# Early chunks load into their own memory, alternate their output banks, and share VectorE with weight conversion in another order

## The chip, the cores and the metric

The kernel runs on one core of one Trainium2 chip. The metric is the device time of one execution in microseconds; the time before is the median of three runs. A profile is one execution recorded by the hardware profiler.

## The reference

All arithmetic must have float32 quality; the weights and vectors of the two dense layers arrive as float64 and are taken apart on the chip.

```python
def _attn_ref(q, k, v, lam):                 # (2, 8, 768, 64), causal decay lam per head
    for b in range(nb):                      # the kernel uses blocks of 128 in place of 64
        intra = einsum('bhic,bhjc->bhij', qb, kb) * Dmask
        intra = einsum('bhij,bhjd->bhid', intra, vb)
        inter = einsum('bhid,bhde->bhie', qb * lam_pow, kv_state)
        out[:, :, sl] = intra + inter
        kv_state = lam_block * kv_state + einsum('bhsd,bhse->bhde', kb * rev_pow, vb)

x = attn_out as 1536 tokens x 512
h = x @ w_in;  x = (h * clip(h + 3, 0, 6) / 6) @ w_out          # layer 1, 512 -> 2048 -> 512
h = x @ w_in;  g = P(h) / (Q(h) + 1e-6);  out = g @ w_out        # layer 2, same shapes
```

## The kernel before, in words

The attention is cut into 12 chunks of 128 tokens (6 to each batch entry). For chunk c, `att_t` transposes q and k on TensorE into two PSUM banks and ScalarE copies them out as qT and kT; GpSimd makes qd (q times its decay) and kd (k times its decay). `att_s` multiplies k by q into two banks, and VectorE multiplies the result by the decay mask into `at`. `att_o` gathers the chunk's output in bank X from state times qd (not in the first chunk of a batch entry) and from at times v, and the new state's addition in bank Y. `att_state` adds that addition to the decayed state on VectorE, and GpSimd makes the decayed copy sd. `att_x` splits the output into a high part xh (ScalarE) and a rest xl (VectorE), both read from bank X.

A dense layer multiplies with weights that are split in the same way into a high part (wih, woh) and a rest (wil, wol). A job of weight conversion has one or two halves of 128x512: `load_job` fetches the raw float64 words; `conv_c` scales on ScalarE (L153) and clips on VectorE (L154); `conv_s` scales the low words on ScalarE (L176) and joins them on VectorE (L177); `conv_w` puts the sign in on VectorE (L194); `conv_h` makes the high part on ScalarE (L207) and the rest on GpSimd (L208). Jobs 0 and 1 have one half each (the weights of `mm1(0)` and `mm1(1)`), and every later job has two: the first half of job 2 is the weight of `mm1(2)`.

`mm1(s)` is 12 TensorE multiplications of 512 columns into hb, of xh by wih (L216), xh by wil (L218) and xl by wih (L220); `act1` (tc on ScalarE, td on VectorE) and `act_fin` (gh on ScalarE, gl on GpSimd) turn it into the input of `mm2(s)`, of four quarters with three multiplications each. The program first does chunks 0 to 3, which fill the first 512 tokens, then the scores of chunk 4 and `mm1(0)`, and then eight steps s = 0 to 7, each of which weaves chunk 4+s into the first layer; then the dense layers alone. The order of the work on each engine is written out by hand, and each engine takes its instructions strictly in that order. Loads wait in SyncE's queue, also in order, until the buffer that they fill is free: q, k and v have two buffers each, raw words two of each kind.

Of the kernel before, what the change touches and what calls it, by code (L numbers as in the profile page):

```python
# [8 lines left out]
F32 = mybir.dt.float32  # L9
# [11 lines left out]
WARM = (6, 2, 3)  # L21
# [9 lines left out]
def fused_kernel(  # L31
# [52 lines left out]
    EIN, EOUT = 11, 9  # L84
    w_tiles(wp, range(EIN), range(EOUT))
# [223 lines left out]
    with ExitStack() as actx:  # L309
        ap = actx.enter_context(tc.tile_pool(name="ap", bufs=1))  # L310
# [13 lines left out]
        def load_nat(c, which):  # L324
            b, s0 = c // CPB, (c % CPB) * CH
            for nm in which:
                x = ap.tile([128, H, D], F32, name=nm + "n", bufs=2)
                src = {"q": q, "k": k, "v": v}[nm]
                nc.sync.dma_start(x, src[b, :, s0 : s0 + CH, :].rearrange("h s d -> s h d"))
                nat.setdefault(c, {})[nm] = x  # L330

        def att_t(c, bk, between=None):
            qn, kn, vn = (nat[c][nm] for nm in "qkv")
# [11 lines left out]
            nc.scalar.copy(kT.rearrange("p a b -> p (a b)"), bk[1])  # L345
            qd = kd = None
# [24 lines left out]
        Xv = X.rearrange("p (a b) -> p a b", a=NP)  # L371
        Yd = Y[:, 0 : 64 * NP].rearrange("p (a b) -> p a b", a=NP)
        decayed = {}

        def att_o(c):
            at, qd, kd, vn = live[c]
            cs = [slice(128 * p, 128 * p + 128) for p in range(NP)]

            if qd is not None:
                for p in range(NP):  # L380
                    nc.tensor.matmul(X[:, cs[p]], lhsT=state[:, p, :], rhs=qd[:, p, :], start=p == 0, stop=False,
# [6 lines left out]
            for p, h2, r in halves:  # L388
                nc.tensor.matmul(X[r, cs[p]], lhsT=vn[:, 2 * p + h2, :], rhs=at[:, h2, p, :],
                                 start=qd is None and p == 0, stop=p == NP - 1, skip_group_check=True)  # L390

        def att_state(c):
            if c % CPB == CPB - 1:
                return
            for h2 in range(2):
# [12 lines left out]
        def att_x(c):  # L408
            del live[c]
            o = CH * (c % CPT)  # L410
# [5 lines left out]
        with tc.manual_schedule():  # L416
            load_nat(0, "qk")
            nc.scalar.dma_start(lamb, lam.unsqueeze(0).to_broadcast([128, H]))
            load_nat(1, "qk")
            load_nat(0, "v")  # L420
            nc.vector.memset(warm, 0.0)
# [11 lines left out]

            warm_up(WARM[0])
            for h2 in range(2):
                r = slice(64 * h2, 64 * h2 + 64)
                nc.vector.tensor_copy(lamq[r, :], lamb.rearrange("p (a b) -> p a b", b=2)[r, :, h2])
            for p in range(NP):
# [3 lines left out]
                for h2 in range(2):  # L442
                    hd = 2 * p + h2
                    nc.vector.tensor_tensor_scan(
                        out=dmat[:, h2, p, :], data0=lamb[:, hd : hd + 1].to_broadcast([128, CH]), data1=ident,
                        initial=0.0, op0=ALU.mult, op1=ALU.add)
            for h2 in range(2):
                nc.vector.tensor_copy(ktab[:, :, h2], dmat[:, h2, :, CH - 1])
# [4 lines left out]


            att_t(0, hb, lambda: warm_up(WARM[1]))
            warm_up(WARM[2])
            load_nat(2, "qk")
            load_nat(1, "v")
            att_s(0, acc[0:2])
            load_job(0)  # L460
            att_t(1, hb)
            att_o(0)
            att_state(0)
            att_x(0)
            load_nat(2, "v")
            load_nat(3, "qk")
            load_job(1)
            att_s(1, acc[2:4])
            att_t(2, hb)
            conv_all(conv_c, 0)  # L470
            conv_all(conv_s, 0)
            conv_all(conv_w, 0)
            att_o(1)
            att_state(1)
            att_x(1)
            conv_all(conv_h, 0)
            load_nat(3, "v")
            load_nat(4, "qk")
            load_job(2)
            att_s(2, acc[0:2])  # L480
            att_t(3, hb)
            conv_all(conv_c, 1)
            conv_all(conv_s, 1)
            conv_all(conv_w, 1)
            att_o(2)
            att_state(2)
            att_x(2)
            conv_all(conv_h, 1)
            load_nat(4, "v")
            load_job(3)  # L490
            load_nat(5, "qk")
# [153 lines left out]
```

## Time and profile before

| what | value |
|---|---|
| three runs, median (lowest to highest) | 602.6 us (602.4 to 602.93) |
| the profiled execution's own time | 602.82 us |
| its span in the profile | 600.9 us, so 1.92 us lie around it |
| TensorE's busy share | 98% |
| granted TensorE clock, mean | 1.0 of full speed |

The span runs from the first to the last record; the time of the execution lies 1.92 us above it. A busy share is an average over the whole span; the change touches the first 115 us or so.

### The profile page before, as it was taken

The page shows a single profiled execution, that of the slowest core. Times are in us where ns is not written, and L with a number is a line of the kernel's source. Part 1 is how long each engine was busy: PE and PEld are TensorE (multiplying, and loading weights), DVE is VectorE, ACT ScalarE, POOL GpSimd, SP SyncE. Part 2 cuts the span into 40 slices and gives each one's busy share as a digit, 9 for nine tenths or more (in the row PEclk, how much of TensorE's full clock was granted, in tenths as well). Part 3 has the DMA queues.
Part 4 walks back from the last instruction along what each step waited for, and adds up shares of the span by engine and source line. Part 5 has one row for each costly group of instructions (what it writes and reads, how often), then busy time and mean ns, then how long its engine had stood idle before and what let it go on. Part 6 is the DMA issues. An engine that isn't in the chain of part 4 may idle for free.

```text
span 600.9 us, 8288 instructions
## 1 busy us (share of the span) xinstructions
PE 588.1 (98%) x3035; PEld 480.6 (80%) x3035; DVE 445.2 (74%) x476; ACT 384.0 (64%) x635; POOL 366.8 (61%) x291
## 2 busy tenths in 40 slices
PE   8898999999999999999999999999999999999997
PEld 5786888888888888888888787877788888888886
DVE  5877888787411011488888899999999888999991
ACT  2566465677422222588787877787887767877771
POOL 3756677566421222266676677688776677777772
PEclk9999999999999999999999999999999999999999
DMA  8987755364000000266655000000010000100001
GB/s 169 267 214 196 173 157 160 130 211 150 1 1 0 1 0 1 88 206 197 184 171 172 1 1 35 1 0 2 28 43 0 2 0 2 69 2 0 1 1 71
DMA packets 61289, 46.68 MB, mean 78 GB/s; under 512 B 39104, under 2 KB 55744, under 8 KB 61248
## 3 DMA queue, kind: packets, MB, share of 16 engines
q1 hardware_dynamic: 60960, 46.02, 26.9%
q8 instruction: 24, 0.39, 0.3%
q10 hardware_dynamic: 288, 0.14, 0.1%
q14 instruction: 17, 0.14, 0.1%
HBM read 43.00 MB, written 3.15 MB: 77 GB/s over the span
## 4 chain that ended last, share of the span: by engine, by line
PE 52%; DVE 24%; ACT 4%; issue 3%; POOL 1%; DVEq 0%; ACTq 0%
PE acc L235 26%; DVE Y L304 8%; PE hb L216 8%; PE hb L220 8%; PE hb L218 8%; DVE ta L154 2%; DVE X L164 2%; DVE ta L194 2%; DVE Y L164 2%; DVE tb L294 2%; DVE tb L194 2%; ACT ta L153 1%; DVE td L305 1%; DVE tb L154 1%; DVE raw L184 1%
## 5 line engine op out<-in xcount | busy, mean ns | idle before, releaser
L304 DVE RECIPROCAL Y<-tb 128x512 f32<-128x512 f32 x48 | 161.3, 3360 | 1.6
L281 POOL TENSOR_TENSOR gl<-td,gh 128x512 fp32r<-128x512 f32 x84 | 111.2, 1324 | 77.1 <-ACT gh L280 76.0
L216 PE MATMUL hb<-xh,wih 128*128 128x512 f32 x384 | 104.3, 393 | 0.5 <-ACT td L293 0.4
L218 PE MATMUL hb<-xh,wil 128*128 128x512 f32 x384 | 102.7, 389 | 0.0
L220 PE MATMUL hb<-xl,wih 128*128 128x512 f32 x384 | 102.6, 389 | 0.0
L295 POOL TENSOR_TENSOR tc<-ta,tc 128x512 f32<-128x512 f32 x48 | 62.2, 1295 | 58.2 <-ACT tc L292 58.2
L271 DVE SCALAR_TENSOR_TENSOR td<-tc,hb 128x512 f32<-128x512 f32 x48 | 32.8, 683 | 84.3 <-ACT tc L268 84.3
L216 PEld LDWEIGHTS hb<-xh,wih 128*128 128x128 f32 x384 | 71.1, 188 | 17.4 <-ACT td L293 1.8
L218 PEld LDWEIGHTS hb<-xh,wil 128*128 128x128 f32 x384 | 72.1, 188 | 15.2
L220 PEld LDWEIGHTS hb<-xl,wih 128*128 128x128 f32 x384 | 72.1, 188 | 15.0
L268 ACT ACTIVATE tc<-hb,c 128x512 f32<-128x512 f32 x48 | 32.9, 686 | 71.7 <-PE hb L220 71.6
L235 PE MATMUL acc<-gh,woh 128*128 128x512 f32 x192 | 76.1, 396 | 0.0
L235 PE MATMUL acc<-gl,woh 128*128 128x512 f32 x192 | 74.8, 390 | 0.0
L235 PE MATMUL acc<-gh,wol 128*128 128x512 f32 x192 | 74.8, 389 | 0.0
L280 ACT CAST gh<-td 128x512 fp32r<-128x512 f32 x84 | 52.0, 619 | 25.9 <-DVE td L271 13.8
L296 POOL TENSOR_TENSOR td<-td,tc 128x512 f32<-128x512 f32 x48 | 63.8, 1330 | 3.8
L208 POOL TENSOR_TENSOR wil<-ta,wih 128x512 fp32r<-128x512 f32 x32 | 41.4, 1294 | 34.7 <-ACT wih L207 34.7
L289 ACT ACTIVATE X<-hb,b_sb 128x512 f32<-128x512 f32 x48 | 31.8, 662 | 42.8 <-PE hb L220 34.1
L235 PE MATMUL acc<-woh,gl 128*128 128x512 f32 x144 | 56.5, 392 | 1.1 <-POOL gl L281 1.1
L235 PE MATMUL acc<-woh,gh 128*128 128x512 f32 x144 | 56.2, 390 | 0.3 <-ACT raw L253 0.3
L235 PE MATMUL acc<-wol,gh 128*128 128x512 f32 x144 | 56.0, 389 | 0.0
L208 POOL TENSOR_TENSOR wol<-tb,woh 128x512 fp32r<-128x512 f32 x29 | 38.4, 1324 | 14.4 <-ACT woh L207 14.4
(104 smaller groups left out, 1029.1 us busy)
## 6 DMA issues: line engine op xcount, KB each, us to landing
raw<-in_moe_w_in_dram SPq DMA_DIRECT2D x32, 512.0 KB, 3.8
raw<-in_moe_w_out_dram SPq DMA_DIRECT2D x32, 512.0 KB, 4.6
qn<-in_q_dram SPq DMA_DIRECT2D x12, 256.0 KB, 5.5
kn<-in_k_dram SPq DMA_DIRECT2D x12, 256.0 KB, 5.3
vn<-in_v_dram SPq DMA_DIRECT2D x12, 256.0 KB, 4.8
out_dram<-raw SPq DMA_DIRECT2D x11, 256.0 KB, 2.2
out_dram<-raw ACTq DMA_DIRECT2D x1, 128.0 KB, 1.8
out_dram<-raw SPq DMA_DIRECT2D x1, 128.0 KB, 1.7
```

The lines of the kernel that those rows point to most:

```text
L208: nc.gpsimd.tensor_tensor(lo, x, hi.bitcast(F32), op=ALU.subtract)
L216: nc.tensor.matmul(h, lhsT=ih[:, kk, :], rhs=xh[tb][:, kk, :], start=kk == 0, stop=False)
L218: nc.tensor.matmul(h, lhsT=il[:, kk, :], rhs=xh[tb][:, kk, :], start=False, stop=False)
L220: nc.tensor.matmul(h, lhsT=ih[:, kk, :], rhs=xl[tb][:, kk, :], start=False, stop=kk == KD - 1)
L235: nc.tensor.matmul(acc[d], lhsT=l, rhs=r, start=st and i == 0, stop=sp and i == 2)
L268: nc.scalar.activation(t, h, AF.Relu, bias=c3)
L271: nc.vector.scalar_tensor_tensor(out=g, in0=t, scalar=6.0, in1=h, op0=ALU.min, op1=ALU.mult)
L280: nc.scalar.copy(gh, g)
L281: nc.gpsimd.tensor_tensor(gl, g, gh.bitcast(F32), op=ALU.subtract)
L295: nc.gpsimd.tensor_tensor(b1, h2, b1, op=ALU.mult)
L296: nc.gpsimd.tensor_tensor(a1, a1, b1, op=ALU.add)
L304: nc.vector.reciprocal(Y, q1)
```

## The change

Three things are altered. The natural q, k and v of chunks 0 to 3 get a buffer each, in a pool `pp` whose memory the weights wi5 to wi10 take over later, so that none of these loads waits for a buffer; they are issued at once, with the raw words of jobs 0 and 1 between them. `att_o` gets its banks as an argument: chunks 0 to 3 put their output alternately into X and Y and into acc[2] and acc[3], and all scores of the early chunks use acc[0] and acc[1]. The order written by hand is altered: jobs 0 to 2 are converted later, in single steps between a chunk's own steps; in the steps s the order becomes `att_x` before `att_state`, only one half of `conv_s` before them, and `conv_w` of a job in the following step, after td and ahead of at. The counts of the start's dummy multiplications (WARM) go from 6, 2, 3 to 8, 3, 2.

```diff
-WARM = (6, 2, 3)
+WARM = (8, 3, 2)
...
-    EIN, EOUT = 11, 9
-    w_tiles(wp, range(EIN), range(EOUT))
+    EARLY, EIN, EOUT = 5, 11, 9
+    w_tiles(wp, range(EARLY), range(EOUT))
+    pre = ExitStack()
+    pp = pre.enter_context(tc.tile_pool(name="pp", bufs=1))
...
-                x = ap.tile([128, H, D], F32, name=nm + "n", bufs=2)
+                if c < CPT:
+                    x = pp.tile([128, H, D], F32, name=f"{nm}n{c}")
+                else:
+                    x = ap.tile([128, H, D], F32, name=nm + "n", bufs=2)
...
-        def att_o(c):
+        def att_o(c, bk=(X, Y)):
...
             load_nat(0, "qk")
             nc.scalar.dma_start(lamb, lam.unsqueeze(0).to_broadcast([128, H]))
-            load_nat(1, "qk")
             load_nat(0, "v")
+            load_nat(1, "qkv")
+            load_nat(2, "qkv")
+            load_job(0)
+            load_nat(3, "qkv")
+            load_job(1)
+            load_nat(4, "qk")
...
+            S, O = acc[0:2], ((X, Y), acc[2:4])
+            slots = {
+                2: ((conv_c, 0), (conv_s, 0)),
+                3: ((conv_w, 0), (conv_c, 1)),
+            }
+            for c in range(CPT):
+                att_s(c, S)
+                att_t(c + 1, hb)
+                for f, j in slots.get(c, ())[0:1]:
+                    conv_all(f, j)
+                att_o(c, O[c % 2])
+                if c < CPT - 1:
+                    att_d(c + 1)
+                    att_state(c)
+                else:
+                    conv_all(conv_h, 0)
+                    att_state(c)
+                    att_d(c + 1)
+                for f, j in slots.get(c, ())[1:2]:
+                    conv_all(f, j)
+                att_x(c)
...
+            conv_all(conv_s, 1)
+            load_nat(6, "qk")
+            att_s(CPT, S)
+            conv_all(conv_w, 1)
+            conv_all(conv_h, 1)
+            load_job(3)
...
                 if s == 0:
                     mm1(0)
                     act1(0)
+                    conv_all(conv_c, 2)
+                    conv_s(2, 0)
                     att_o(c)
-                    att_state(c)
                     att_x(c)
+                    att_state(c)
+                    conv_s(2, 1)
+                    conv_all(conv_w, 2)
                     act_fin(0)
-                    conv_all(conv_c, j)
-                    conv_all(conv_s, j)
+                    conv_all(conv_h, 2)
...
+                    att_d(c)
+                    conv_all(conv_w, j - 1)
+                    conv_all(conv_h, j - 1)
...
                     conv_all(conv_c, j)
-                    conv_all(conv_s, j)
+                    conv_s(j, 0)
                     mm2(s - 1, (2, 3))
                     att_o(c)
-                    att_state(c)
                     att_x(c)
-                    conv_all(conv_w, j)
+                    att_state(c)
+                    conv_s(j, 1)
```

The part of `att_t` that made qd and kd is now the function `att_d`, and the new pool that holds wi5 to wi10 opens after `pre.close()`.

On VectorE, this is the place from the scores of chunk 4 to the sign step of job 2 (ta and tb are the two halves of a job), before the change:

```order
L366 TENSOR_TENSOR at<-acc_78,dmat 128x512
L366 TENSOR_TENSOR at<-acc_79,dmat 128x512
L398 TENSOR_TENSOR state<-sd,Y 64x4x64 x2
L414 TENSOR_TENSOR xl_87<-X,xh_84 128x4x128
L154 TENSOR_SCALAR ta<-ta 128x512
L154 TENSOR_SCALAR tb<-tb 128x512
L177 SCALAR_TENSOR_TENSOR ta<-ta,raw_340 128x512
L177 SCALAR_TENSOR_TENSOR tb<-tb,raw_342 128x512
L366 TENSOR_TENSOR at<-acc_76,dmat 128x512
L366 TENSOR_TENSOR at<-acc_77,dmat 128x512
L194 SCALAR_TENSOR_TENSOR ta<-raw_340,ta 128x512
L194 SCALAR_TENSOR_TENSOR tb<-raw_342,tb 128x512
```

It runs from chunk 3's at to job 2's sign steps. After the change, from job 1's sign step (raw_167) on, it reads:

```order
L196 SCALAR_TENSOR_TENSOR ta<-raw_167,ta 128x512
L273 SCALAR_TENSOR_TENSOR td<-tc,hb_80 128x512
L156 TENSOR_SCALAR ta<-ta 128x512
L156 TENSOR_SCALAR tb<-tb 128x512
L179 SCALAR_TENSOR_TENSOR ta<-ta,raw_327 128x512
L426 TENSOR_TENSOR xl_88<-X,xh_85 128x4x128
L409 TENSOR_TENSOR state<-sd,Y 64x4x64 x2
L179 SCALAR_TENSOR_TENSOR tb<-tb,raw_329 128x512
L196 SCALAR_TENSOR_TENSOR ta<-raw_327,ta 128x512
L196 SCALAR_TENSOR_TENSOR tb<-raw_329,tb 128x512
```

Job 2 (raw_327, raw_329) now stands behind td of `mm1(0)`, and chunk 4's xl and state (xl_88) stand inside it.

On ScalarE at the same place, after the change; wih_92 is job 1's high part, wih_94 that of job 2, hb_80 the result of `mm1(0)` and hb_81 that of `mm1(1)`:

```order
L209 CAST wih_92<-ta 128x512
L270 ACTIVATE tc<-hb_80,c_121 128x512
L155 ACTIVATE ta<-raw_327 128x512
L155 ACTIVATE tb<-raw_329 128x512
L178 ACTIVATE raw_327<-raw_327 128x512
L425 CAST xh_85<-X 128x4x128
L178 ACTIVATE raw_329<-raw_329 128x512
L282 CAST gh<-td 128x512
L569 ACTIVATE b1a<-b_sb 128x1
L209 CAST wih_94<-ta 128x512
```

Before the change job 2's four steps on raw words stood ahead of tc, behind wih_92 and the copies of chunks 4 and 3; now they stand behind tc.

On VectorE in a later step (from the mask product of chunk 7 to that of chunk 8; its job is raw_682 and raw_684, or raw_729 and raw_731 after the change), first before the change:

```order
L366 TENSOR_TENSOR at<-Y,dmat 128x512
L154 TENSOR_SCALAR ta<-ta 128x512
L154 TENSOR_SCALAR tb<-tb 128x512
L177 SCALAR_TENSOR_TENSOR ta<-ta,raw_682 128x512
L177 SCALAR_TENSOR_TENSOR tb<-tb,raw_684 128x512
L398 TENSOR_TENSOR state<-sd,Y 64x4x64 x2
L414 TENSOR_TENSOR xl_88<-X,xh_85 128x4x128
L194 SCALAR_TENSOR_TENSOR ta<-raw_682,ta 128x512
L194 SCALAR_TENSOR_TENSOR tb<-raw_684,tb 128x512
L271 SCALAR_TENSOR_TENSOR td<-tc,hb_81 128x512
L366 TENSOR_TENSOR at<-X,dmat 128x512
```

And the same place after the change:

```order
L375 TENSOR_TENSOR at<-Y,dmat 128x512
L156 TENSOR_SCALAR ta<-ta 128x512
L156 TENSOR_SCALAR tb<-tb 128x512
L179 SCALAR_TENSOR_TENSOR ta<-ta,raw_729 128x512
L426 TENSOR_TENSOR xl_88<-X,xh_85 128x4x128
L409 TENSOR_TENSOR state<-sd,Y 64x4x64 x2
L179 SCALAR_TENSOR_TENSOR tb<-tb,raw_731 128x512
L273 SCALAR_TENSOR_TENSOR td<-tc,hb_81 128x512
L196 SCALAR_TENSOR_TENSOR ta<-raw_729,ta 128x512
L196 SCALAR_TENSOR_TENSOR tb<-raw_731,tb 128x512
L375 TENSOR_TENSOR at<-X,dmat 128x512
```

xl now has one joining step fewer and no state ahead of it; the two sign steps have moved from ahead of td to between td and at.

## Rows read from the trace of the kernel before

**Rows 1.** Busy time by step, s=3 and s=6 (window: length, PE, PEld, DVE, ACT, POOL).

```profile
61.44:71.81 10.37, 10.37 (x90) 8.56 (x89) 8.79 (x14) 6.06 (x11) 7.05 (x6) 1.00 0.75 185
...
93.01:103.86 10.85, 10.58 (x91) 8.54 (x89) 9.28 (x13) 6.17 (x11) 7.80 (x7) 1.00 0.49 136
```

**Rows 2.** TensorE rows with a wait, from the timeline: start us, us, what ended it.

```profile
28.00 1.13 PE L381 MATMUL X<-qd,state 128*128 128x128 f32 x8 [1.78 <-DVE xl L414]
...
48.41 1.13 PE L381 MATMUL X<-qd,state 128*128 128x128 f32 x8 [0.58 <-DVE at L366]
...
54.75 0.66 PE L339 MATMUL X<-ident,qn 128*128 128x128 f32 x4 [1.24 <-DVE xl L414]
```

**Rows 3.** The scores of chunks 1 and 2 on TensorE, from the timeline.

```profile
13.40 1.26 PE L362 MATMUL acc<-qT,kT 64*128 64x128 f32 x16
...
18.00 1.26 PE L362 MATMUL acc<-qT,kT 64*128 64x128 f32 x16
```

**Rows 4.** TensorE after the four chunks, from the timeline.

```profile
31.74 1.19 PE L216 MATMUL hb<-xh,wih 128*128 128x512 f32 x4
...
34.60 1.05 PE L381 MATMUL X<-qd,state 128*128 128x128 f32 x8
...
39.92 1.07 PE L216 MATMUL hb<-xh,wih 128*128 128x512 f32 x4
...
42.65 0.60 PE L339 MATMUL X<-ident,qn 128*128 128x128 f32 x4
```

**Rows 5.** VectorE's single steps near chunk 4, from the timeline.

```profile
29.86 0.87 DVE L398 TENSOR_TENSOR state<-sd,Y 64x256 f32<-64x256 f32 x2 [0.81 <-PE Y L386]
...
31.28 0.69 DVE L414 TENSOR_TENSOR xl<-X,xh 128x512 fp32r<-128x512 f32 x1 [0.55 <-ACT xh L413]
...
32.99 0.41 DVE L154 TENSOR_SCALAR tb<-tb 128x512 f32<-128x512 f32 x1
...
33.33 0.68 DVE L177 SCALAR_TENSOR_TENSOR ta<-ta,raw 128x512 uint32<-128x512 uint32 x1
...
34.53 1.28 DVE L366 TENSOR_TENSOR at<-acc,dmat 128x512 f32<-128x512 f32 x2
```

**Rows 6.** Job 2's first half: scaling, sign step, high part, from the timeline.

```profile
31.14 0.70 ACT L153 ACTIVATE ta<-raw 128x512 f32<-128x512 f32 x1
...
35.73 0.68 DVE L194 SCALAR_TENSOR_TENSOR ta<-raw,ta 128x512 uint32<-128x512 uint32 x1
...
36.44 0.62 ACT L207 CAST wih<-ta 128x512 fp32r<-128x512 f32 x1 [2.91 <-DVE ta L194]
```

**Rows 7.** VectorE and GpSimd side by side in chunk 3, from the timeline.

```profile
22.90 1.46 POOL L349 TENSOR_TENSOR qd<-qT,qtab 128x512 f32<-128x512 f32 x1
...
23.32 1.59 DVE L177 SCALAR_TENSOR_TENSOR ta<-ta,raw 128x512 uint32<-128x512 uint32 x1
...
24.33 1.49 POOL L352 TENSOR_TENSOR kd<-kn,ktab 128x512 f32<-128x512 f32 x1
...
24.95 1.42 DVE L194 SCALAR_TENSOR_TENSOR ta<-raw,ta 128x512 uint32<-128x512 uint32 x1
```

**Rows 8.** The start of step s=3 on three engines, from the timeline.

```profile
64.56 0.69 ACT L268 ACTIVATE tc<-hb,c 128x512 f32<-128x512 f32 x1 [2.42 <-PE hb L220]
...
65.72 0.67 DVE L271 SCALAR_TENSOR_TENSOR td<-tc,hb 128x512 f32<-128x512 f32 x1
...
65.81 1.29 POOL L349 TENSOR_TENSOR qd<-qT,qtab 128x512 f32<-128x512 f32 x1 [1.16 <-ACT qT L340]
...
67.93 0.69 DVE L366 TENSOR_TENSOR at<-X,dmat 128x512 f32<-128x512 f32 x1 [1.53 <-PE Y L362]
```

**Rows 9.** The first loads of all, issued until 45 us: rate by slice of 1.1 us, and landing.

```profile
GB/s 0 47 127 198 249 224 222 218 118 0 199 262 264 322 245 181 191 162 351 259 219 219 323 401 311 267 352 379 277 185 60 209 241 218 105 376 427 260 15 0
...
raw<-in_moe_w_in_dram SPq DMA_DIRECT2D x5, 512.0 KB, 5.1
```

**Rows 10.** The last dummy multiplications of the start, from the timeline.

```profile
7.84 1.49 PE L432 MATMUL Y<-warm 128*128 128x512 bf16 x3
```

More of the change, by code (lines that the diff above doesn't have):

```diff
@@ L309, in fused_kernel @@
     with ExitStack() as actx:
-        ap = actx.enter_context(tc.tile_pool(name="ap", bufs=1))
+        ap = actx.enter_context(tc.tile_pool(name="ap", bufs=1, side="right"))
         lamb = ap.tile([128, H], F32, name="lamb")
@@ L332, in att_t @@
         def att_t(c, bk, between=None):
-            qn, kn, vn = (nat[c][nm] for nm in "qkv")
+            qn, kn = (nat[c][nm] for nm in "qk")
             qT = ap.tile([128, NP, CH], F32, name="qT")
@@ L345, in att_t, with att_d @@
             nc.scalar.copy(kT.rearrange("p a b -> p (a b)"), bk[1])
+            live[c] = qT, kT
+        def att_d(c):
+            (qT, kT), (kn, vn) = live[c], (nat[c][nm] for nm in "kv")
             qd = kd = None
@@ L380, in att_o @@
                 for p in range(NP):
-                    nc.tensor.matmul(X[:, cs[p]], lhsT=state[:, p, :], rhs=qd[:, p, :], start=p == 0, stop=False,
+                    nc.tensor.matmul(ox[:, cs[p]], lhsT=state[:, p, :], rhs=qd[:, p, :], start=p == 0, stop=False,
                                      skip_group_check=True)
@@ L394, in att_state @@
                 return
+            Yd = outs[c][1]
             for h2 in range(2):
@@ L409, in att_x @@
             del live[c]
+            Xv = outs[c][0]
             o = CH * (c % CPT)
@@ L434, in fused_kernel @@
             warm_up(WARM[0])
+            for hd in range(H):
+                nc.vector.tensor_tensor_scan(
+                    out=dmat[:, hd % 2, hd // 2, :], data0=lamb[:, hd : hd + 1].to_broadcast([128, CH]), data1=ident,
+                    initial=0.0, op0=ALU.mult, op1=ALU.add)
+            for h2 in range(2):
+                nc.vector.tensor_copy(ktab[:, :, h2], dmat[:, h2, :, CH - 1])
             for h2 in range(2):
@@ L441, in fused_kernel @@
                     initial=1.0, op0=ALU.mult, op1=ALU.add)
[L442 to L448, printed above, removed]
             def conv_all(f, j, *a):
@@ L540, in fused_kernel @@
                     conv_all(conv_c, j)
-                    conv_all(conv_s, j)
+                    conv_s(j, 0)
                     mm2(s - 1, (2, 3))
                     att_o(c)
+                    att_x(c)
                     att_state(c)
-                    att_x(c)
-                    conv_all(conv_w, j)
+                    conv_s(j, 1)
                 if c + 2 < NCH:
                     load_nat(c + 2, "v")
+            conv_all(conv_w, j)
             conv_all(conv_h, j)
-    wq = ctx.enter_context(tc.tile_pool(name="wq", bufs=1))
+    wq = ctx.enter_context(tc.tile_pool(name="wq", bufs=1, side="right"))
     w_tiles(wq, range(EIN, NF), range(EOUT, NF))
```

75 lines of the change are left out of this document (20 added, 55 removed).

## The prediction

> **What bounds the kernel now.** I read the page first: TensorE is busy in 98% of the span at its full granted clock, so a gain has to be a wait or a gap taken out of TensorE. The busy time by step says where any are left. A full step with a chunk in it takes 10.37 us when TensorE never waits, and 10.85 where it does [rows 1]; from the row at 61.44 to the end of the row at 93.01 are four such steps, 42.42 us together, so they lose 42.42 - 4 x 10.37 = 0.94 us. VectorE is busy for 8.8 to 9.3 us of each: it is the next limit, and it matters in which order its work stands.
>
> The timeline of TensorE then names the waits. Three carry the argument: 1.78 us in chunk 3, until xl has read bank X; 0.58 us in step s=1, until at is there; 1.24 us at the start of s=2, for bank X again [rows 2]. A chunk that waits for nothing goes from scores to scores in 18.00 - 13.40 = 4.60 us [rows 3]. `mm1(0)` begins at 31.74 and takes 2.86 until chunk 4's output; that and `mm1(1)` take 5.32 together, `mm1(2)` takes 2.73, and step s=1 begins at 42.65 [rows 4].
>
> Last I laid VectorE and GpSimd side by side. A joining step of 0.68 us alone [rows 5] took 1.59 in chunk 3, ending where GpSimd's qd let go; the next GpSimd operation then waited for it, and the sign step behind took 1.42 in place of 0.68 [rows 6, 7]. So the clip, joining and sign steps of a conversion and any GpSimd operation exclude each other, and where both have work they take turns. The mask product at, xl, td and state do not show this.
>
> **The change part by part.**
>
> *The front.* With own buffers the loads wait for nothing but the rate, and odd chunks no longer wait for bank X. The loads of 256 KB came at about 0.22 MB/us, the wider raw words at 0.25 to 0.4 [rows 9]; q and k of chunk 4, fifteenth in the queue, then land about 23 us, just when TensorE wants them. If chunk 1's scores stay at 13.40 (the dummies between the first loads and these scores are five either way), chunk 4's scores begin at 13.40 + 3 x 4.60 = 27.20, and `mm1(0)`, behind scores of 1.26 [rows 3], at about 28.4, where it was 31.74. It ends at 31.25. That is 3.3 us gained, if it lasted.
>
> *Job 2.* `mm1(2)` is the third multiplication of its kind and needs job 2's first half. Before, the scaling of this half began at 31.14, ahead of tc of `mm1(0)`, and its high part came at 36.44 to 37.06 [rows 6]; `mm1(2)` wanted it at 39.92, so nearly 3 us lay between. Now the whole job stands behind td of `mm1(0)`. I add up VectorE from the at of chunk 3, which can begin about 24.6 (chunk 2's output ends at 22.6, then xh 0.58, xl 0.69, and a joining step held by GpSimd). Up to job 1's sign step there are two mask products (2.56), two sign steps (1.36), state (0.87), a clip (0.41), xl (0.69) and a joining step (0.68) [rows 5, 6]: 6.56 us, so 31.2. Three of these meet job 0's rest, sd and the scaling of job 1 under way; I take 1.3 us of waits for them, about one GpSimd operation [rows 8]: 32.5. ScalarE takes its queue in order: job 1's high part 0.62, then only tc 0.69 [rows 6, 8]; td 0.67 more: 34.5. Then clips with a short hold (1.0), a joining step (0.68): 36.2; xl and state 1.56: 37.75; the second joining step behind gl of `mm1(0)` (0.7 of hold and 0.65): 39.1; the sign step 0.65: 39.75; high part 0.62: 40.4.
>
> TensorE is ready before that. Its chunk 4 output waits for qd and kd, which GpSimd makes behind job 0's rest and sd: some 4.6 us of operations from 27.3 on, and 1.7 us in which VectorE's steps come between, so kd ends at 33.6 and the output at about 35.05; `mm1(1)` ends at 37.9. So `mm1(2)` waits 2.5 us for the high part, another 0.4 for the rest (1.29 on GpSimd, against 0.93 of TensorE's work over it), and ends at 43.65 where it ended at 42.65. **Term: +1.0.** Without a single hold the same chain is 2.3 us shorter (1.3, 0.3 and 0.7), which gives -1.3; with one more GpSimd operation in it (kd ahead of job 1's sign step, about 1 us: in rows 7 it takes 0.91 from the end of the joining step on) it gives +2.0. I stay with one hold each, since GpSimd has an operation ready at nearly every moment of this stretch.
>
> *Step s=1.* Its sign steps stood between td and at before as well: this is the 0.58 us of rows 2. New is that gl of `mm1(1)` goes ahead of qd, so that qd (1.29 [rows 8]) falls among the sign steps; half of it shows: **+0.65**, between 0 and +1.0.
>
> *Step s=2.* The 1.24 us for bank X [rows 2] lose a joining step (0.68) ahead of xl, while kd of the next chunk goes between. **-0.2**, between -0.7 and 0.
>
> *Steps s=3 to s=6.* Ahead of xl, a joining step (0.68) and state (0.87) are gone, so the 0.94 us that these steps lose now can come back. Against it the sign steps move in ahead of at. VectorE idles 1.53 us there [rows 8], and two sign steps take 1.36. But tc ends at 65.25, td would end at 65.92 if nothing stood before it, and qd has begun at 65.81: the first sign step is held until 67.10, runs to 67.75, lets kd through (0.9), and the second ends at 69.4. at then begins at 69.4 and not 67.93. TensorE has six multiplications of 2.73/12 us [rows 4] to do from 67.93 on, needs bank X back at 69.3, and gets it behind the first product (0.69) at 70.1, a wait of some 0.75. Further on ScalarE casts the second high part, and scales the next job, 3 us later than now, which takes up part of what xl gained. In full it costs 4 x 0.75 = 3 us; in the next step sd runs late and the sign step can come first, so I take 2.1 less the 0.94: **+1.2**, between -0.94 and +3. Step s=7 has no kd and no state: 0.
>
> The rest of the edits cost nothing: behind s=7 the conversions stand where they stood, under a TensorE that is busy nearly throughout. The raw words of job j+1 go behind two more loads in SyncE's queue, 3 us later; with 5.1 us to landing [rows 9] they are there before the next step, 10 us on. Cover gone, each us late is one lost.
>
> **Sum.** 1.0 + 0.65 - 0.2 + 1.2 = +2.65 on the profiled execution's 602.82 (its span of 600.9 and 1.92 around it), so 605.5; that execution lies 0.2 above the median of the runs, so 605.3. The lowest terms give -2.9 (599.9), the highest +6.0 (608.8).
>
> **The rivals.**
>
> *Bank X decides (faster).* In the early part GpSimd's operations fall beside the chain and not into it, and in the steps the sign pair fits into the 1.53 us. For it: td misses qd's start by only 0.1 us, so if qd comes a little later the sign step goes first and at is on time. It decides at one point: whether the first sign step of a step starts before qd. Then the steps return 0.94 and s=2 0.7, and the front keeps up to 1.25: 600 to 601.4.
>
> *Give and take.* The front's +1.0 stands, but the steps return what rows 1 lose: 602.82 + 1.0 - 0.2 - 0.94 is 602.7; with the spread of the terms 601.4 to 603.8.
>
> *The raw words of job 2 come late (much slower).* Their buffer is free only after job 0's sign step, at about 26.6, while the transfer could be issued some 5 us sooner before. With 5.1 us to landing and the two halves one behind the other they are there by 32 to 33.5; they are wanted at 33.8. From there each us late is a us more: 607 to 610.
>
> *The dummies.* The last three, of 512 columns, took 1.49 us, where four later multiplications of 512 columns take 1.07 [rows 4, 10]: the start runs at the lower level, 1.2 GHz, and not 2.4. If the changed dummies brought the rise sooner, chunk 0 would begin up to 1 us earlier, and all behind it: 604.3. The Trainium skill (TensorE: Matmul & The Clock Gate, section What's actually happening) says that the array starts at half its clock and that sustained activity releases it, which speaks for this; by that rule, two more dummies ahead and a shorter pause would bring the rise forward. Against it: the pause before the first load stays, and the number of dummies after it too.
>
> **How the numbers follow.** About 0.2% (1.2 us) is what a measurement of this kernel can tell from no change. My forecast has 0.45, late loads 0.05, the dummies 0.05: slower 0.55. Bank X decides: 0.28, faster. Give and take: 0.17, same. The time is that of the forecast, 605.3. Between 600.0 and 608.7 lie all but the ends of the faster case and of the late loads. Slower alone: 604 to 608.7.
>
> **What would show it.** Right: `mm1(0)` at about 28.4, then a wait of `mm1(2)` for the high part of 1 to 3 us, step s=1 at 43 to 45; in s=3 to s=6, waits of the chunk's output for at, and steps of about 10.7 to 11.3 us. Wrong: a `mm1(2)` that starts right behind `mm1(1)`, or steps of 10.4 us with the sign steps done before the scores end.

## The result and the profile after

The changed kernel takes 608.59 us (median of 4 runs, 606.92 to 608.78), the kernel before 602.59 on the same chip (4 runs): a ratio of 1.0093, with a 95% interval of 1.0075 to 1.0111. The forecast was 605.3. The sign and the range held, but the loss is 6.0 us where 2.7 were expected. Of the four executions of the changed kernel three, with a mean granted clock of 0.995 to 0.997, took 608.58 to 608.78, and one, with 1.0, took 606.92. The profiled execution of the changed kernel took 608.78 us, its span 606.9, against 602.82 and 600.9 before.

The first view is TensorE's timeline, with the rows that answer to [rows 2], [rows 4] and [rows 10]: start us, us, instruction, and in brackets the wait ahead of it.

```profile
6.80 0.60 PE L349 MATMUL hb<-ident,kn 128*128 128x128 f32 x4
7.24 0.59 PE L449 MATMUL Y<-warm 128*128 128x512 bf16 x2
8.08 1.26 PE L371 MATMUL acc<-qT,kT 64*128 64x128 f32 x16 [0.24 <-ACT kT L350]
...
18.55 0.66 PE L344 MATMUL hb<-ident,qn 128*128 128x128 f32 x4 [0.72 <-DMA qn<-in_q_dram]
...
29.02 1.20 PE L218 MATMUL hb<-xh,wih 128*128 128x512 f32 x4
...
31.87 1.05 PE L391 MATMUL X<-qd,state 128*128 128x128 f32 x8
...
39.82 1.64 PE L218 MATMUL hb<-xh,wih 128*128 128x512 f32 x4 [2.26 <-ACT wih L209]
41.27 2.00 PE L220 MATMUL hb<-xh,wil 128*128 128x512 f32 x4
43.07 1.43 PE L222 MATMUL hb<-xl,wih 128*128 128x512 f32 x4
44.33 0.60 PE L344 MATMUL X<-ident,qn 128*128 128x128 f32 x4
...
50.98 1.13 PE L391 MATMUL X<-qd,state 128*128 128x128 f32 x8 [1.44 <-DVE at L375]
...
53.07 1.20 PE L218 MATMUL hb<-xh,wih 128*128 128x512 f32 x4
```

The early part is faster: chunk 0's scores begin at 8.08, `mm1(0)` at 29.02 where it was 31.74, and the 1.78 us for bank X in chunk 3 are gone. Then `mm1(2)` waits 2.26 us for job 2's high part, and not only that: it takes 44.33 - 39.82 = 4.51 us, where it took 2.73. The table of windows says why; its columns are the window, then its length, the busy times of PE, PEld, DVE, ACT and POOL, the granted clock (PEclk), and the DMA share and rate.

```profile
38.00:40.00 2.00, 0.18 (x1) 0.18 (x2) 1.72 (x3) 0.85 (x2) 0.15 (x1) 1.00 1.07 330
40.00:42.00 2.00, 2.00 (x6) 1.35 (x7) 1.00 (x2) 2.00 (x4) 2.00 (x2) 0.59 0.84 213
42.00:44.00 2.00, 2.00 (x6) 1.58 (x6) 2.00 (x4) 1.26 (x3) 0.39 (x1) 0.56 1.06 382
44.00:46.00 2.00, 2.00 (x15) 1.72 (x14) 0.21 (x1) 1.04 (x3) 0.00 (x0) 1.00 0.46 102
```

The clock falls behind the wait: in the two stretches from 40 to 44 us it is 0.59 and 0.56, so TensorE runs mostly at its lower level, 1.2 GHz. So the wait is paid twice, once while it lasts and once behind it. The execution with a mean clock of 1.0 took 1.7 us less than the other three; there is no trace of it, so that it is this fall that it lacks is likely and not shown. The chain that leads to it, from the timeline of VectorE, ScalarE and GpSimd, is the one that the prediction added up:

```profile
32.64 0.68 ACT L270 ACTIVATE tc<-hb,c 128x512 f32<-128x512 f32 x1
33.35 0.69 DVE L273 SCALAR_TENSOR_TENSOR td<-tc,hb 128x512 f32<-128x512 f32 x1 [1.27 <-ACT tc L270]
...
36.69 1.28 POOL L283 TENSOR_TENSOR gl<-td,gh 128x512 fp32r<-128x512 f32 x1 [2.46 <-ACT gh L282]
37.17 1.35 DVE L179 SCALAR_TENSOR_TENSOR tb<-tb,raw 128x512 uint32<-128x512 uint32 x1
38.44 0.68 DVE L196 SCALAR_TENSOR_TENSOR ta<-raw,ta 128x512 uint32<-128x512 uint32 x1
...
39.15 0.62 ACT L209 CAST wih<-ta 128x512 fp32r<-128x512 f32 x1 [2.44 <-DVE ta L196]
```

The second joining step is held by gl of `mm1(0)` and takes 1.35; the sign step and the high part follow it. Next come the steps s=3 and s=6, against [rows 1], from the same kind of windows:

```profile
63.13:74.19 11.06, 10.68 (x91) 8.54 (x89) 9.34 (x13) 6.32 (x11) 8.08 (x6) 1.00 0.50 129
...
96.16:107.12 10.96, 10.64 (x91) 8.54 (x89) 9.95 (x13) 6.32 (x11) 8.57 (x7) 1.00 0.53 161
```

All four steps from s=3 on now take about 11 us: 43.99 together, where they were 42.42. The start of s=3 on three engines, against [rows 8]:

```profile
67.09 0.69 DVE L273 SCALAR_TENSOR_TENSOR td<-tc,hb 128x512 f32<-128x512 f32 x1 [1.04 <-ACT tc L270]
...
67.60 1.29 POOL L358 TENSOR_TENSOR qd<-qT,qtab 128x512 f32<-128x512 f32 x1 [0.65 <-ACT qT L345]
...
67.69 1.74 DVE L196 SCALAR_TENSOR_TENSOR ta<-raw,ta 128x512 uint32<-128x512 uint32 x1
...
69.36 1.53 DVE L196 SCALAR_TENSOR_TENSOR tb<-raw,tb 128x512 uint32<-128x512 uint32 x1
...
69.59 0.50 PE L237 MATMUL acc<-gh,woh 128*128 128x512 f32 x1
...
70.81 0.68 DVE L375 TENSOR_TENSOR at<-X,dmat 128x512 f32<-128x512 f32 x1
...
71.64 1.13 PE L391 MATMUL X<-qd,state 128*128 128x128 f32 x8 [0.38 <-DVE at L375]
```

Two sign steps of 0.68 alone take 1.74 and 1.53 beside qd and kd, at begins at 70.81, and the chunk's output waits for it. From the second half of `mm2` to the chunk's output go 71.64 - 69.59 = 2.05 us, in place of 69.34 - 67.86 = 1.48 before:

```profile
67.86 0.50 PE L235 MATMUL acc<-gh,woh 128*128 128x512 f32 x1
...
69.34 1.05 PE L381 MATMUL X<-qd,state 128*128 128x128 f32 x8
```

The rest is seen only when the starts of `mm1(s)` are laid beside those of before. The lag, in us:

| place | lag | since the row above |
|---|---|---|
| `mm1(0)` | -2.72 | |
| `mm1(2)` | -0.10 | +2.62 |
| step s=1 (its first transposes) | +1.68 | +1.78 |
| `mm1(3)` | +2.57 | +0.89 |
| `mm1(4)` | +1.69 | -0.88 |
| `mm1(8)` | +3.26 | +1.57 |
| `mm1(9)` | +3.11 | -0.15 |
| s=95 | +4.98 | +1.87 |
| last multiplication (602.32, before 596.85) | +5.47 | +0.49 |
| end of the span (606.88, before 600.95) | +5.93 | +0.46 |

Half of the loss arises before `mm1(9)`; the other half comes where the kernels do the same work in the same order without a new wait. It doesn't come evenly: the lag stands still over most of the time and grows in the passes that use late weights (wi11 to wi15, wo9 to wo15): by 0.03 to 0.05 us in each of the first 48 passes that does, and by 0.08 to 0.16 us in each from s=76 to s=83, where wo is the streaming operand. At s=50, 64 and 67 together 0.96 us come back, at places where TensorE waited 0.26 to 0.37 us before the change and now waits little or not at all. In the built kernels these weights have other addresses: their pool is now at the right side of SBUF, 704 bytes further up.

### The profile page after: what moved, and what is told of

Same layout as the page of the kernel before. It is cut to its first block, busy times and chain, and to the rows that moved or that the text cites. A ratio compares the mean times of both kernels' runs of the same rounds, so it can differ in the third digit from the quotient of the medians.

```text
span 606.9 us, 8292 instructions
## 1 busy us (share of the span) xinstructions
PE 592.7 (98%) x3037; PEld 481.0 (79%) x3037; DVE 450.9 (74%) x476; ACT 385.7 (64%) x635; POOL 373.2 (61%) x291
## 4 chain that ended last, share of the span: by engine, by line
PE 59%; DVE 26%; ACT 5%; issue 4%; SPq 3%; DMA 1%; POOL 1%; DVEq 0%; ACTq 0%
PE acc L237 27%; PE hb L218 9%; PE hb L220 9%; PE hb L222 9%; DVE Y L306 8%; DVE ta L156 3%; SPq L334 2%; DVE ta L196 2%; DVE tb L196 2%; DVE X L166 2%; ACT ta L155 2%; DVE Y L166 2%; DVE tb L296 2%; DVE td L307 1%; DVE tb L156 1%
## 5 line engine op out<-in xcount | busy, mean ns | idle before, releaser
L220 PE MATMUL hb<-xh,wil 128*128 128x512 f32 x384 | 104.2, 393 | 0.0
L210 POOL TENSOR_TENSOR wil<-ta,wih 128x512 fp32r<-128x512 f32 x32 | 43.7, 1365 | 34.4 <-ACT wih L209 34.4
```

Of the source, the lines that this page charges most:

```text
L210: nc.gpsimd.tensor_tensor(lo, x, hi.bitcast(F32), op=ALU.subtract)
L220: nc.tensor.matmul(h, lhsT=il[:, kk, :], rhs=xh[tb][:, kk, :], start=False, stop=False)
```

## Experiments

Times below are medians; each ratio is against the kernel before on the same chip, 602.6 to 602.8 each time. Lags are those of the profiled execution, as in the table. Runs whose programs are the same up to `mm1(0)` differ there by up to 0.7 us (the kernel before and its variants) and 1.2 us (the changed kernel and its variants), so a lag is read by where it changes.

**The late weights back at the left side (e1).** The changed kernel with one word less, so that the late weights have their old addresses:

```diff
-    wq = ctx.enter_context(tc.tile_pool(name="wq", bufs=1, side="right"))
+    wq = ctx.enter_context(tc.tile_pool(name="wq", bufs=1))
```

> Theory P (place): the late weights (wi11 to wi15, wo9 to wo15) now lie 704 bytes further up in every partition than before the change, and TensorE reads them more slowly; put back to their old addresses, the lag on the kernel before stops growing behind the eight steps, where it is 3.1 us, so the run takes about 605.7 us, and a dense step with late weights takes 5.44 us again and not 5.49. Rival C (clock): the later steps are slower for another reason, such as what the wait of mm1(2) does to the clock; then the run stays at 608.6 and the steps at 5.49.

606.09 us, ratio 1.0046 [1.0034, 1.0058]: 2.5 us of the 6.0 are gone. The lag is 3.44 at s=9, 3.49 at s=95, and 3.49 still at the last multiplication. So the growth hangs on the pool's place. From s=9 to the last multiplication the lag grows by 2.35 us in the changed kernel and by 0.05 here; these 2.3 us are the firmer price, since medians of so few executions move by some tenths.

**The place alone (g1).** The kernel before with that one word added:

```diff
-    wq = ctx.enter_context(tc.tile_pool(name="wq", bufs=1))
+    wq = ctx.enter_context(tc.tile_pool(name="wq", bufs=1, side="right"))
```

> The kernel before with one word changed: the late weights (wi11 to wi15, wo9 to wo15) are taken from the other end of SBUF, so they get the addresses that they have in the changed kernel, and no instruction moves. Placement theory: only multiplications that read late weights take longer, about 0.05 us per four steps of 5.5 us and 0.0068 us per multiplication in the tail; the start up to step s=9 is unchanged, the lag grows in the passes over late weights, and the whole takes 2.5 to 2.9 us more: 605.1 to 605.5. Rival: the growth came from the granted clock of the changed kernel's runs (0.997 against 1.0) and not from the addresses: 602.6, no change.

605.1 us, 1.0043 [1.0027, 1.0058], with a mean granted clock of 1.0 in three of the four executions: the placement theory holds. From s=9 to the last multiplication the lag grows by 2.31 us. The starts of four passes on TensorE's timeline show it, s=10 to s=13; late weights come into use with s=11:

```profile
119.07 1.07 PE L216 MATMUL hb<-xh,wih 128*128 128x512 f32 x4
...
124.51 1.08 PE L216 MATMUL hb<-xh,wih 128*128 128x512 f32 x4
...
130.00 1.08 PE L216 MATMUL hb<-xh,wih 128*128 128x512 f32 x4
...
135.49 1.08 PE L216 MATMUL hb<-xh,wih 128*128 128x512 f32 x4
```

A pass takes 5.44 us with early weights, 5.49 with late ones, with no wait in either: the same multiplications are 1% slower.

**Which address is slow (h1, h2).** In the kernel before, padding between the late weights gives each pair an offset of its own against the old place:

```diff
-    w_tiles(wq, range(EIN, NF), range(EOUT, NF))
+    for i, f in enumerate(range(EOUT, NF)):
+        if i:
+            wq.tile([128, 24], F32, name=f"pad{f}")
+        w_tiles(wq, (), (f,))
+    wq.tile([128, 32], F32, name="padi")
+    w_tiles(wq, range(EIN, NF), ())
```

The last pad has 128 bytes, so all wi stand at 704 and not at the 672 that the expectation names. h2 does the same for wi, with pads of 160 bytes.

> The kernel before with no instruction moved; the late output weights (wo9 to wo15) stand 0, 96, 192, 288, 384, 480 and 576 bytes further up than where a whole number of 2048-byte tiles would put them, the late input weights all 672 bytes. If what costs is a particular remainder of the address (32 bytes over a multiple of 128 is what the fast placement has), the passes over f grow unevenly: none at offset 0 and 384, most at the others, 601 to 602 in the span plus the usual 1.9. If any distance from the old place costs alike, every pass from the second offset on grows by about 0.03 us for the output weights. If the cost begins at one offset, the passes show the place. If it is not the offset within 2048 bytes but the place as a whole, nothing of a pattern is seen.

> The same with the late input weights (wi11 to wi15) 0, 160, 320, 480 and 640 bytes further up, and the output weights all 704. Output weights alone: seven passes of +0.03 us each in every round over the weights; input weights add 0.02 us at the offsets that cost and nothing at the others. Whole: 604 to 605.2.

One timed execution each: 605.4 and 606.1 us, above the 602.9 to 603.9 and the 604 to 605.2 that were expected. The half passes of h1, from the starts on the timeline (12 multiplications with wo each):

```profile
133.22 0.39 PE L235 MATMUL acc<-gh,woh 128*128 128x512 f32 x1
...
136.03 1.09 PE L216 MATMUL hb<-xh,wih 128*128 128x512 f32 x4
...
138.79 0.39 PE L235 MATMUL acc<-gh,woh 128*128 128x512 f32 x1
...
141.53 1.08 PE L216 MATMUL hb<-xh,wih 128*128 128x512 f32 x4
...
144.29 0.39 PE L235 MATMUL acc<-gh,woh 128*128 128x512 f32 x1
...
147.08 1.08 PE L216 MATMUL hb<-xh,wih 128*128 128x512 f32 x4
```

Offset 96 gives 136.03 - 133.22 = 2.81 us, offset 192 gives 2.74, offset 288 gives 2.79. In full: wo at 0, 96, 192, 288, 384, 480, 576 takes 2.72, 2.81, 2.74, 2.79, 2.79, 2.79, 2.80; wi at 0, 160, 320, 480, 640 (h2) takes 2.72, 2.80, 2.80, 2.80, 2.79; wi at 704 (h1) 2.74 to 2.77. Up to 0.03 spills into the half pass behind. Of my cases none fits: not "none at 0 and 384", since 384 is slow, and not "any distance costs alike", since 192 and 704, which are 512 apart, cost less than half of what the others do. The changed kernel happened to get a mild one.

**All operands moved together (i1, i2).** One padding tile ahead of everything in the kernel before, of 64 and of 224 bytes (56 elements):

```diff
+    const.tile([128, 16], F32, name="pad")
     c3 = const.tile([128, 1], F32, name="c3")
```

Before, the weights and the activations xh, xl, gh, gl all start at the same remainder (288 modulo 512). The two runs ask whether that remainder matters, or only that it is shared.

> The kernel before with 64 bytes of padding ahead of everything in SBUF: weights, activations and early buffers all stand 64 bytes further up, so all operands of the multiplications still share one remainder modulo 512 (352 in place of 288), and no instruction moves. If two operands of a multiplication must share the remainder, nothing changes: passes of 5.44 us throughout, 602.4 to 603. If 288 itself is the good remainder, every pass takes 0.1 to 0.16 us more, as those with shifted weights did: 88 passes or so, 612 or more.

> The same with 224 bytes, so that all these operands start at a multiple of 512 bytes. Shared remainder: 602.4 to 603, as before. If starting at a multiple of 512 is better than any shared remainder, passes shorter than 5.44 us and less than 602; if only 288 is good, 612 or more.

602.55 us, 0.9999 [0.9989, 1.0008], and 602.56 us, 1.0 [0.999, 1.0009]. With late weights in use the passes of i1 still are 5.44 apart:

```profile
124.25 1.07 PE L217 MATMUL hb<-xh,wih 128*128 128x512 f32 x4
...
129.69 1.07 PE L217 MATMUL hb<-xh,wih 128*128 128x512 f32 x4
...
135.13 1.07 PE L217 MATMUL hb<-xh,wih 128*128 128x512 f32 x4
```

So none of the three remainders (288, 352 and 0) is good or bad by itself: a multiplication is fast when its two operands share the remainder. That it is the two operands that must agree is the nearest reading, but i1 and i2 moved other tiles along with them. That the modulus is 512 rests on 192 and 704 alone; in all these kernels the fast operands agree modulo 2048, the length of a tile, as well, and a distance of just 512 wasn't run.

**The order inside the steps as before (e2).** In the changed kernel the conversions of s=1 to s=7 go back to their old places:

```diff
                     if s == 1:
                         att_t(c, (X, Y))
+                        att_d(c)
                         act_fin(1)
                         act1(s + 1)
+                        conv_all(conv_w, j - 1)
                     else:
                         act1(s + 1, lambda: att_t(c, (X, Y)))
-                    att_d(c)
-                    conv_all(conv_w, j - 1)
+                        att_d(c)
                     conv_all(conv_h, j - 1)
...
-                    conv_s(j, 0)
+                    conv_all(conv_s, j)
...
-                    att_x(c)
                     att_state(c)
-                    conv_s(j, 1)
+                    att_x(c)
+                    conv_all(conv_w, j)
...
-            conv_all(conv_w, j)
```

> Only the order inside the steps s=1 to s=7 is put back (both joining steps and state ahead of xl, sign steps at the step's end, qd ahead of gl in s=1). Theory S, as the prediction has it: the sign steps ahead of at cost more than the earlier xl gives back; from the start of mm1(3) to that of mm1(9) the changed kernel takes 63.98 us, and with the old order it takes 63.4, mm1(3) comes 0.6 to 0.9 us earlier in s=1, so the run takes about 607.5 us. Rival: the new order in the steps is the better one, and the run takes 609 to 610 us.

606.73 us, 1.006 [1.0048, 1.0072]. The lag at `mm1(9)` is 1.45 in place of 3.11. In the list of TensorE's waits (us in total, times, longest) bank X is back, and the waits for at fall from 2.8 us to 0.5:

```profile
PE X L344 <- DVE xl L426: 1.3, 1, 1.3
...
PE X L391 <- DVE at L375: 0.5, 1, 0.5
```

The new order of the steps costs 1.66 us; counted from the start of step s=1 it is 1.64.

**TensorE kept at work while `mm1(2)` waits (e3).** Nine dummy multiplications ahead of `mm1(2)`, into a bank that is free; no work of the reference is left out:

```diff
+                    if s == 1:
+                        for i in range(9):
+                            nc.tensor.matmul(acc[3], lhsT=warm[:, 0:128], rhs=warm, start=True, stop=True)
                     mm1(s + 1)
```

> Nine dummy multiplications of 512 columns, into a bank that nobody reads then, stand ahead of mm1(2) and fill its wait of 2.3 us. Theory C: it is the empty stretch on TensorE that takes the clock down to its lower level for the 12 multiplications of mm1(2), which took 4.5 us and not 2.7; filled, they take 2.8, and the run takes 606.9 to 607.2 us, as the one run of the changed kernel at full granted clock did. Rival: mm1(2) is slow because its weights come late (the rest, wil, ends 1.3 us behind the high part); then it takes 4 us with the dummies as well, and the run stays at 608.6.

607.14 us, 1.0068 [1.0056, 1.008]. The high part still comes when it comes, but the granted clock is 1.00 in every window from 34 to 44 us, and `mm1(2)` takes 42.43 - 39.11 = 3.32 us, a wait for the low part included:

```profile
36.66 2.12 PE L538 MATMUL acc<-warm 128*128 128x512 bf16 x9
39.11 1.20 PE L218 MATMUL hb<-xh,wih 128*128 128x512 f32 x4 [0.33 <-ACT wih L209]
40.48 1.19 PE L220 MATMUL hb<-xh,wil 128*128 128x512 f32 x4 [0.17 <-POOL wil L210]
...
42.43 0.60 PE L344 MATMUL X<-ident,qn 128*128 128x128 f32 x4
```

Work without use brings 1.45 us by the medians, and `mm1(2)` itself is 1.2 us shorter. (The lag of `mm1(3)` falls by 1.9, but 0.8 of it stands already at `mm1(0)`.) So the fall of the clock, and not the wait alone, is a cause by itself. All five executions have a mean clock of 0.999 or 1.0, and their median is no better than the 606.92 of the changed kernel's one execution with 1.0: the dummies seem to pay only where the clock would fall.

**Job 2's first half to its end first (e4), and the same with the old steps and the old place (h4).** In the changed kernel, both halves of job 2 are no longer taken through each stage together:

```diff
-                    conv_s(2, 1)
-                    conv_all(conv_w, 2)
+                    conv_w(2, 0)
+                    conv_h(2, 0)
+                    conv_s(2, 1)
+                    conv_w(2, 1)
                     act_fin(0)
-                    conv_all(conv_h, 2)
+                    conv_h(2, 1)
```

> In step s=0 the first half of job 2 is finished (sign step, high part, rest) before the second half is joined. Theory J, as the prediction has it: mm1(2) waits only for this half; its high part comes some 1.3 us earlier (a joining step held by gl of mm1(0) stands behind it and not ahead), the wait falls from 2.3 to about 1 us, mm1(2) keeps the full clock, and the run takes 605.5 to 607.5 us. Rival: the wait moves to the second half, which mm2(0) needs, or to ScalarE's tc of mm1(1), and the run stays within 0.5 us of 608.6.

> The changed kernel with late weights at their old addresses, the steps s=1 to s=7 in the order of the kernel before, and job 2's first half prepared to its end ahead of its second half. If the late conversions of job 2 are the front's only cost, mm1(2) at 38.2 to 38.6 without a wait over 1 us, step s=1 at 41.5 to 42.5, and 602 to 603. Rival: VectorE has the same work to do whatever its order, so what mm1(2) gains the next chunk loses (scores, at or the clipped low part late): 604 to 605.5.

e4: 609.87 us, 1.0114 [1.0101, 1.0127]. h4: 605.41, 1.0042 [1.0027, 1.0057]. `mm1(2)` begins 1.6 us sooner than in the changed kernel, at 38.22 and 38.10, and step s=1 at 41.57 and 41.43, 1.1 to 1.2 us ahead of the kernel before; but `mm1(3)` is later than there by 3.96 and 1.79. The waits of e4 say where it went:

```profile
PE X L391 <- DVE at L375: 3.4, 5, 2.0
...
PE X L371 <- ACT kT L350: 1.0, 1, 1.0
PE acc L237 <- POOL wol L210: 0.9, 1, 0.9
PE hb L218 <- ACT wih L209: 0.8, 1, 0.8
```

The 2.3 us for wih turned into waits of the next step for kT, for the low part wol and for at. `mm1(2)` keeps the full clock in both; in e4 it falls later, behind the wait of 2.0 us for at (0.50 from 52 to 54 us). The rival's mechanism held both times: an earlier first half only makes the rest late. Its time held for h4; e4 came out 0.8 us above it.

**The three undone together (g2).** The changed kernel with the edits of e1, e2 and e3.

> The changed kernel with three things undone together: late weights at their old addresses, the order inside steps s=1 to s=7 as before, and TensorE kept at work (nine dummies) while mm1(2) waits for job 2. If the three causes add (2.5 + 1.9 + 1.5 us of the 6.0): 602.4 to 603.0, and step s=1 begins within 0.3 us of the kernel before. Rival: they overlap, the wait only moves from the steps to another place: 604 or more.

603.38 us, 1.0008 [0.9999, 1.0017]: within measurement of the kernel before, 5.2 us under the changed one, and 0.4 above the range that was expected. `mm1(3)` lags by 0.53 and `mm1(9)` by 0.25. One by one the three are worth 2.50 + 1.86 + 1.45 = 5.8 by the medians, so they overlap a little if at all. About 0.5 us of what is left lies behind the last multiplication, as in e1 and in every other kernel with the changed early part (4.5 to 4.6 us to the end of the span, 4.1 before). The last two transfers take the same 1.8 and 1.7 us there. The difference lies behind them: the last one lands 1.53 us ahead of the end of the span, 1.08 before, and only the closing instructions of the engines follow. Why these take longer stays open.

**Parts of the early change alone.** g3 takes the early loads, the banks and the dummies, with the conversions, the steps and the late weights as before. h3 is the kernel before with the changed banks alone (one line of the four calls stands here), g4 the kernel before with the changed dummies alone:

```diff
-            att_s(3, acc[2:4])
+            att_s(3, acc[0:2])
...
-WARM = (6, 2, 3)
+WARM = (8, 3, 2)
```

> The changed kernel's front alone: early loads into buffers of their own, outputs in alternate banks, the changed dummies; the conversions stand where they stood in the kernel before (job 2 ahead of the products of mm1(0)), so do the steps, and the late weights keep their old addresses. If the front's gain survives when job 2 is not late: mm1(0) at 28.5 to 29.5 in place of 31.74, no wait for the high part of job 2 over 0.5 us, and 600.5 to 601.5. Rival: VectorE is the limit in the front, and the conversions ahead of the products only move the wait into the output of chunk 4 or mm1(2): 602 to 603, no gain.

> The kernel before with only the banks changed: scores of chunks 0 to 3 all in the first pair, outputs of odd chunks in the second pair. The 1.78 us wait of chunk 3 for bank X goes. If VectorE is the limit of the front, chunk 3 then waits for state or at behind job 1's conversions, mm1(0) moves by less than 0.5 us and the time stays at 602.2 to 602.8. Rival: the bank was the limit, mm1(0) comes 1 to 1.8 us earlier, and 601 to 601.8 if step s=1 keeps it.

> The kernel before with the numbers of dummies 8, 3, 2 in place of 6, 2, 3. If they alone bring the rise of the clock forward: k's transposes of chunk 0 at 0.6 us each in place of 1.09, the scores of chunk 0 about 1.2 us earlier; the loads of before then bind chunk 1 or bank X chunk 3, so 601.4 to 602.3 if a part is kept, 602.6 if none. Rival: the rise came from the earlier loads and not from the dummies: nothing moves, 602.6.

g3: 603.02 us, 1.0004 [0.9995, 1.0013]. h3: 602.69, 1.0 [0.9991, 1.001]. Neither gains: in both, chunk 3 no longer waits for bank X, and waits about as long (1.76 and 1.49 us) for state, which stands on VectorE behind the conversion of job 1. From g3's timeline:

```profile
27.48 1.13 PE L391 MATMUL acc<-qd,state 128*128 128x128 f32 x8 [1.76 <-DVE state L409]
```

g4: 603.6, 1.0013 [1.0004, 1.0022]: no gain, if anything a loss. Chunk 0's scores do begin sooner, at 8.35 against 9.26 (8.6 to 9.0 in the other runs with the old dummies). Then TensorE waits 1.08 us for q of chunk 3 and 1.03 for bank X, and in the profiled execution the clock falls, which costs more than was won (`mm1(0)` +0.85):

```profile
18.00:20.00 2.00, 0.95 (x7) 0.71 (x8) 1.83 (x4) 0.99 (x3) 0.00 (x0) 1.00 0.90 185
20.00:22.00 2.00, 0.97 (x7) 0.76 (x6) 1.96 (x5) 1.38 (x3) 1.33 (x2) 0.70 1.16 318
22.00:24.00 2.00, 2.00 (x19) 1.78 (x20) 1.54 (x3) 1.25 (x2) 2.00 (x2) 0.50 1.26 214
```

No version ran measurably faster than the kernel before.

## Why the prediction was right in sign and wrong in size

**The step that failed is "The rest of the edits cost nothing: behind s=7 the conversions stand where they stood".** It counted instructions and waits, and found none. The edit to the pool's side moved no instruction, but it moved the late weights by 704 bytes, and that costs 2.4 to 2.5 us of the 6.0 by the medians of e1 and g1, and 2.3 by their traces. No rival held it either. What stands ahead of the prediction names three alterations and the first 115 us; the pool's side is a fourth, its line is not among those shown there, and it reaches to the last pass. Such an edit shows in neither the order nor the waits of before; the addresses would have shown it, had I compared them, but not its price. Another 0.5 us at the end of the span belong to the same missing remainder, and are unexplained.

The signs that the prediction named all came: `mm1(0)` at 29.02, a wait of 2.26 us, step s=1 at 44.33, steps of about 11 us with waits for at. They could not show the miss, since none lies behind the steps. That the range held, by 0.1 us, is luck: its upper end was made of a costlier job 2 and costlier steps, and the time came near it through terms that the sum did not have.

**Job 2: the mechanism was right, the term mis-sized.** The high part was forecast to be there at 40.4 and was at 39.77; the wait was forecast at 2.5 and was 2.26. But the term had the waits alone. `mm1(2)` took 4.51 us where it had 2.73 and 0.4 for the low part, so 1.4 us stood in no term; e3, at full clock, takes 3.32, so the fall of the clock is 1.2 us of it. Step s=1 began at 44.33 and not at 43.65 (the prediction's own 40.4, 0.4 and 2.73 make 43.5). The excess is only 0.7, because the high part came 0.6 sooner. The raw words were not late: the scaling of the half follows tc on ScalarE without a wait.

**The front.** "`mm1(0)` at about 28.4" was 29.02, by two errors against each other. The scores of chunk 1 did not stay at 13.40, since the mechanism of the rival "The dummies" was at work: chunk 0's four transposes of k take 0.60 us, and chunk 1's scores begin at 11.96. The Trainium skill (TensorE: Matmul & The Clock Gate, section What's actually happening) has sustained activity release the clock; this trace agrees (0.60 us for the four where it was 1.06, and 0.66 in g4 with the dummies alone), and so do the scores of chunk 0, at 8.08 and 8.35 where they were at 9.26. What came sooner was then lost to the loads, which the prediction left at "nothing but the rate": waits of 0.72, 0.50 and 0.33 us for q and k of later chunks. Buffers of their own moved these loads little: q of chunk 3 landed at 18.50 where it landed at 19.35 before, and k of chunk 4 at 24.81 and not at about 23. From 5 to 24.6 us the transfers moved 226 GB/s, where they had moved 215 before, so there was little to win. The 1 us that this rival took off the time was not there: g4, the dummies alone, is no faster than before.

**The steps were forecast well.** s=1: +0.65 forecast, +0.89 measured. s=2: -0.2 and -0.88; the wait for bank X fell from 1.24 to 0.36, so a joining step out of the way counted in full. s=3 to s=6: +1.2 and +1.57; td missed qd's start again (67.78 against 67.60), the sign step was held, and each of the four steps lost about 0.6 us, where 0.75 was forecast for most of them. s=7: 0 and -0.15. Together +1.65 and +1.43, and e2, which undoes them, gives 1.66 at `mm1(9)`. The rival "Bank X decides" fell at just the point that it named, since in s=3 to s=6 no first sign step was through before qd; and "Give and take" fell with it, since these steps returned nothing.

Up to `mm1(9)` the sum is so +2.65 forecast and +3.11 measured, with the 1.4 us of `mm1(2)` mostly balanced by a job 2 that came 0.6 sooner and a step s=2 that came out 0.7 better. Most of what is missing lies behind it.

**Why the early loads bring nothing.** The 2.7 us at `mm1(0)` exist, but they come with the later conversions (g3, with these in their old places, has 0.2), and VectorE has the same work to do up to step s=1 in any order: where the conversions stand early (g3, h3), state and at are late; where they stand late (the changed kernel), job 2 is; where its first half is brought forward (e4, h4), the next step is. That VectorE sets the pace is argued from these waits and not shown: from 5 to 44.33 us it is busy for 28.7 to 31.1 of 39.3 us in all these kernels, and waits for other engines in the rest.

## What to carry to other kernels

An early gain on one engine lasts only if the engine behind it has room: before counting it, add up what VectorE must have done by the point where TensorE next waits for it. Price a new wait of TensorE with what the clock loses behind it, and look at PEclk around it; a few useless multiplications can be cheaper, where the clock would fall. When an edit moves a pool, compare the addresses too, and keep the two operands of a multiplication at one remainder; e1 restored that by the old place. Padding should do it too: a pad by itself cost nothing measurable (i1, i2), but no run restored a remainder with one.

## What the runs showed of the hardware that was not expected

TensorE's speed depends on how its two operands stand to each other in SBUF: with the weights as the stationary operand, 2.72 us for 12 multiplications of 512 columns with a shared remainder, 2.74 to 2.77 at distances of 192 and 704 bytes, 2.79 to 2.81 at the other eight tried, with the clock at 1.00. The Trainium skill (SBUF — State Buffer, section Who interferes with whom) gives TensorE two independent read ports, one for the moving operand and one for weight loads, and allows contention at the pair that VectorE and GpSimd share alone. By that rule a common shift and a relative one would cost alike, nothing; the runs differ (i1 and i2: none, h1 and h2: up to 3%), and the measurement decides. Which of the reads collide wasn't shown.

The clock fell after one wait of 2.26 us, in e4 after one of 2.0 us and, in g4, around two of about 1 us close together, but not after single waits of 1.78 us [rows 2] or 1.76 us (g3). And one of the four executions of the changed kernel has a mean clock of 1.0. The length of a wait alone does not tell whether it will fall.
